# One V chunk per row kept in PSUM between the two passes of a decode kernel (GQA attention and MLP, twice)

## Chip, cores, metric

The kernel runs on one core of a Trainium2 chip. The metric is the device time of one execution in microseconds (us). The kernel before took 1153.25 us (median of 4 runs, 1149.37 to 1156.13).

## The reference, cut to what matters

```
B, Sq, D = 8, 1, 448;  Hq, Hkv, Sk, Dh = 16, 8, 4096, 256
x = x + A(layernorm(x), k_cache, v_cache, wq, wo)   # attention over the cache
x = x + Bmlp(layernorm(x), ...)
x = x + A(layernorm(x), k_cache, v_cache, wq, wo)   # the same cache again
x = x + Bmlp(layernorm(x), ...)
```

One K cache and one V cache of 8 rows x 8 heads x 4096 x 256 in bf16 are used twice, with another x. A row's K or V is 16.8 MB, more than the 15 slots (15.7 MB) that the kernel has beside the weights, so most of the cache is read from HBM twice. What a kernel can keep of a row between its first and second pass need not be read again. Here a chunk is 1.049 MB (128 partitions x 4096 bf16); a row has four head pairs `gp`, each with four K and four V chunks.

## The kernel before

Terms: PE is the matrix engine (PEld its weight loads), DVE the vector engine, ACT the scalar engine, SPq the queue that issues the loads. SBUF is the on-chip memory that loads land in, PSUM the banks that PE writes its sums to. "Scores" is q times K, PV the softmax weights times V; pass 0 and pass 1 are the two attentions over a row.

The kernel has 15 chunk slots in SBUF. Eleven chunks of a row stay there between the passes; the tasks of neighbouring rows are interleaved so that pass 1 of row b runs shortly after its kept chunks were loaded.

```python
NC = 15
kept = [(GP - 1, kv, n) for n in range(4) for kv in range(2)] + [(GP - 2, 0, n) for n in range(3)]
...
for b in range(Bn):
    tasks += [(1, b, gp) for gp in keep[::-1]]         # pass 1, pairs 3, 2: frees the kept slots
    if b + 1 < Bn:
        tasks += [(0, b + 1, gp) for gp in keep]       # pass 0, pairs 2, 3: fills them again
    ...
    tasks += [(1, b, gp) for gp in free]               # pairs 0, 1: four slots rotate
    if b + 2 < Bn:
        tasks += [(0, b + 2, gp) for gp in free]       # (cut: the first and last rows differ)
```

The chunks are handled one after the other, K chunk c of task n beside V chunk c of the task before. A slot is given to the next load in order as soon as its chunk has been used:

```python
if kv == 0:
    if not (ps == 1 and stays(it)):
        transpose_k(slot)            # two DVE transposes, 128x1024 uint32, in place
    step(idx)                        # a piece of a row's chain: wo, MLP, next q
    scores(sc_t[n % 2], slot, c, st["q"], gp)
    ...
    if c == 3:
        exps(p_n, sc_t[n % 2], st["z"], gp)     # one exp over a whole score bank
else:
    pv(st["o"], slot, c, gp, begin=...)         # st["o"]: one of three output banks
if not (ps == 0 and stays(it)):
    places.append(p)
emit_loads()
```

All eight PSUM banks are in use: two for scores, three for outputs, `misc`, and two for the sums of the rows' chains.

## Time and profile before

Lines of the page: first the busy time of an engine (share of the span, instructions), then the rate in 40 equal slices of the span, the DMA queue's packets, bytes and share, the bytes from HBM, and the chain of work that ended last, by engine and by line.

```profile
span 1149.6 us, 36707 instructions
PE 705.3 (61%) x17177; PEld 514.0 (45%) x17177; DVE 548.2 (48%) x904; ACT 113.9 (10%) x234; POOL 15.6 (1%) x25
...
GB/s 352 375 420 420 407 385 399 418 412 383 414 420 400 385 399 419 420 403 406 409 420 420 400 400 413 420 420 387 402 412 420 408 371 412 420 410 355 410 420 153
...
q1 hardware_dynamic: 68198, 455.19, 98.0%
...
HBM read 455.15 MB, written 0.01 MB: 396 GB/s over the span
...
DMA 69%; PE 13%; DVE 11%; SPq 3%; issue 2%; POOL 1%; ACT 0%; POOLq 0%; DVEq 0%; ACTq 0%
...
slot<-in_A_v_cache_dram SPq DMA_DIRECT2D x224, 1024.0 KB, 12.3
slot<-in_A_k_cache_dram SPq DMA_DIRECT2D x200, 1024.0 KB, 16.4
```

No compute engine is near full, the queue's packets fill 98% of the span, and the chain is DMA for 69% of it. The rate, however, swings: about 420 GB/s, then down to 371 to 414, once per row (about 137 us, five slices). The same as windows around row 3: the first from the first scores of pass 1, pair 3, to those of pair 1, the second from there to the next row's. The columns are the window, its length, the engines' busy time, the granted clock, the DMA share and GB/s.

```profile
562.60:637.40 74.80, 43.65 (x1072) 30.00 (x1073) 32.88 (x37) 8.52 (x17) 0.00 (x0) 0.57 1.01 418
637.40:699.40 62.00, 42.09 (x970) 31.14 (x969) 33.75 (x69) 5.56 (x12) 1.25 (x2) 0.50 1.00 398
```

I call them the deep and the shallow stretch. In the deep one the kept slots come free one after the other and loads run ahead; in the shallow one 11 slots are held and four rotate. Counted from the issues and landings in the trace (a landing that isn't recorded is taken from its neighbours), up to 8 loads are in flight in row 3's deep stretch and 3 or 4 in its shallow one. The Trainium skill ("HBM Reference", section "Specifications") gives about 425 GB/s for a core that streams alone; the 416 to 426 of this trace's deep 10 us windows agree. My reading of the shallow rate, which e7 and e10 below test, is that the four slots' own cycle sets it. Four pieces of the chain that ended last, in order of time (start, length, what):

```profile
660.56 6.98 DMA slot<-in_A_k_cache_dram
667.56 2.38 DVE slot L547 x2
...
670.63 7.78 DMA slot<-in_A_k_cache_dram
678.43 2.37 DVE slot L547 x2
```

A K load lands 6.98 us after its issue, the two transposes take 2.38, the scores' rest and the semaphores 0.69 (667.56 + 2.38 to 670.63), and then the next load goes into a free slot. One turn is 10.07 us. Four chunks in 10.07 us would be 417 GB/s; any further delay of PE or DVE in the turn lowers that: 398 GB/s, the rate of this stretch, is a turn of 10.5 us on average.

The groups that matter for the change (line, engine, operation, tiles, shapes, count; busy us, mean ns; idle before it and what ended that):

```profile
L547 DVE STREAM_TRANSPOSE slot<-slot 128x1024 uint32<-128x1024 uint32 x400 | 472.7, 1222 | 383.7 <-DMA slot<-in_A_k_cache_dram 375.0
L555 PE MATMUL sc<-slot,qbd 128*8 128x128 bf16 x8192 | 280.6, 286 | 345.6 <-DVE slot L547 287.2
...
L564 ACT ACTIVATE p_n<-sc 128x512 bf16<-128x512 f32 x64 | 84.7, 1323 | 780.6 <-PE sc L555 780.6
...
L381 PE MATMUL misc<-zm,one 128*128 128x8 f32 (+1 forms) x66 | 18.1, 348 | 6.7 <-ACT ptw L584 6.7
```

The DVE waits for K loads (375.0 us), the scores for the DVE. In the last line the z matmul waits for an ACT copy of other columns of `misc`: in this program a wait covers the PSUM bank as a whole.

### The profile page before, as it was taken

What the parts mean: (1) busy time and instruction counts of PE and PEld (TensorE: products, weight loads), DVE (VectorE), ACT (ScalarE), POOL (GpSimd) and SP (SyncE); (2) the same over time, 40 slices, a digit from 0 to 9 for tenths busy, and PEclk for the clock granted to TensorE, in tenths of its full rate; (3) what the DMA queues carried; (4) which work ended last, traced back from release to release, by engine and by line L of the source; (5) the groups of instructions that cost most, each with busy time, mean ns of one, the idle gap of its engine ahead of it and who ended that gap; (6) DMA issues with size and microseconds to landing.
All of it is one profiled execution on the core that took longest, in us unless ns stands there. A gap on an engine that the chain in (4) does not pass through costs nothing.

```text
span 1149.6 us, 36707 instructions
## 1 busy us (share of the span) xinstructions
PE 705.3 (61%) x17177; PEld 514.0 (45%) x17177; DVE 548.2 (48%) x904; ACT 113.9 (10%) x234; POOL 15.6 (1%) x25
## 2 busy tenths in 40 slices
PE   3144677457755667456764676646665576647787
PEld 2023455345533455344542454425443365425666
DVE  5145453455354544546254553445534553445352
ACT  0001011100110011001110101010011001100100
POOL 0000000000000000000000000000000000000000
PEclk9999997655655556555565557555575556555655
DMA  9999999999999999999999999999999999999993
GB/s 352 375 420 420 407 385 399 418 412 383 414 420 400 385 399 419 420 403 406 409 420 420 400 400 413 420 420 387 402 412 420 408 371 412 420 410 355 410 420 153
DMA packets 68349, 457.52 MB, mean 398 GB/s; under 512 B 6999, under 2 KB 13030, under 8 KB 13542
## 3 DMA queue, kind: packets, MB, share of 16 engines
q1 hardware_dynamic: 68198, 455.19, 98.0%
q8 instruction: 134, 2.20, 0.8%
q14 instruction: 17, 0.14, 0.0%
HBM read 455.15 MB, written 0.01 MB: 396 GB/s over the span
## 4 chain that ended last, share of the span: by engine, by line
DMA 69%; PE 13%; DVE 11%; SPq 3%; issue 2%; POOL 1%; ACT 0%; POOLq 0%; DVEq 0%; ACTq 0%
DMA slot<-in_A_k_cache_dram 62%; DVE slot L547 9%; DMA slot<-in_A_v_cache_dram 6%; PE sc L555 4%; PE o L596 3%; PE y_ps L318 2%; SPq L148 2%; PE q_ps L274 1%; DMA wq_sb<-in_A_wq_dram 1%; SPq L539 1%; PE o L610 1%; DVE qbd L300 1%; PE o L318 1%; PE h_ps L336 0%; PE misc L381 0%
## 5 line engine op out<-in xcount | busy, mean ns | idle before, releaser
L547 DVE STREAM_TRANSPOSE slot<-slot 128x1024 uint32<-128x1024 uint32 x400 | 472.7, 1222 | 383.7 <-DMA slot<-in_A_k_cache_dram 375.0
L555 PE MATMUL sc<-slot,qbd 128*8 128x128 bf16 x8192 | 280.6, 286 | 345.6 <-DVE slot L547 287.2
L555 PEld LDWEIGHTS <-qbd 128*8 128x8 bf16 x8192 | 194.5, 105 | 430.8 <-issue 298.6
L596 PE MATMUL o<-slot,ptw 128*8 128x256 bf16 x3968 | 242.8, 388 | 55.8 <-DMA slot<-in_A_v_cache_dram 33.9
L564 ACT ACTIVATE p_n<-sc 128x512 bf16<-128x512 f32 x64 | 84.7, 1323 | 780.6 <-PE sc L555 780.6
L596 PEld LDWEIGHTS <-ptw 128*8 128x8 bf16 x3968 | 107.9, 109 | 93.8 <-issue 45.0
L318 PEld LDWEIGHTS <-wo_sb 128*128 128x128 bf16 (+1 forms) x1600 | 64.8, 124 | 16.2 <-issue 15.6
L318 PE MATMUL y_ps<-OT,wo_sb 128*128 128x1 bf16 (+1 forms) x1280 | 55.5, 177 | 1.5 <-issue 1.5
L384 DVE RECIPROCAL rz<-misc 128x8 f32<-128x8 f32 (+1 forms) x33 | 6.4, 193 | 96.3 <-PE misc L381 96.3
L274 PEld LDWEIGHTS <-wq_sb 128*128 128x128 bf16 x1152 | 33.9, 104 | 19.1 <-issue 17.3
L274 PE MATMUL q_ps<-xb,wq_sb 128*128 128x1 bf16 (+1 forms) x1152 | 35.3, 166 | 11.4 <-DMA wq_sb<-in_A_wq_dram 3.6
L584 ACT CAST ptw<-misc 128x128 bf16<-128x128 f32 x64 | 17.5, 274 | 211.9 <-PE misc L577 159.4
L411 PEld LDWEIGHTS misc<-R,o_sb 128*128 128x128 f32 x124 | 25.9, 293 | 11.0 <-issue 11.0
L318 PEld LDWEIGHTS <-w_sb 128*128 128x128 bf16 (+1 forms) x630 | 25.7, 125 | 7.3 <-issue 5.2
L411 PE MATMUL misc<-R,o_sb 128*128 128x8 f32 x124 | 28.8, 343 | 0.0
L232 POOL TENSOR_TENSOR t<-t,nhalf 128x2 f32<-128x2 f32 (+1 forms) x17 | 10.7, 630 | 1075.8 <-DVE t L239 978.0
L318 PE MATMUL y_ps<-HT_t,w_sb 128*128 128x1 bf16 (+1 forms) x560 | 24.2, 177 | 0.5 <-DVE HT_t L359 0.5
L300 DVE TENSOR_SCALAR qbd<-misc,quad 128x64 bf16<-128x64 f32 x64 | 13.8, 278 | 22.0 <-PE misc L294 22.0
L381 PE MATMUL misc<-zm,one 128*128 128x8 f32 (+1 forms) x66 | 18.1, 348 | 6.7 <-ACT ptw L584 6.7
L336 PEld LDWEIGHTS <-w_sb 128*128 128x128 bf16 x560 | 17.2, 105 | 9.6 <-issue 9.2
L336 PE MATMUL h_ps<-xb,w_sb 128*128 128x1 bf16 (+1 forms) x560 | 17.9, 166 | 4.9 <-DVE xb L249 4.6
L381 PEld LDWEIGHTS misc<-zm,one 128*128 128x128 f32 x66 | 15.2, 287 | 11.9 <-ACT ptw L584 8.4
(92 smaller groups left out, 207.7 us busy)
## 6 DMA issues: line engine op xcount, KB each, us to landing
slot<-in_A_v_cache_dram SPq DMA_DIRECT2D x224, 1024.0 KB, 12.3
slot<-in_A_k_cache_dram SPq DMA_DIRECT2D x200, 1024.0 KB, 16.4
wo_sb<-in_A_wo_dram SPq DMA_DIRECT2D x1, 3584.0 KB, 26.6
wq_sb<-in_A_wq_dram SPq DMA_DIRECT2D x3, 1024.0 KB, 7.0
w_sb<-in_B_w_dram SPq DMA_DIRECT2D x1, 1568.0 KB, 12.8
w_sb<-in_B_w_dram SPq DMA_DIRECT2D x3, 448.0 KB, 26.8
wq_sb<-in_A_wq_dram SPq DMA_DIRECT2D x2, 256.0 KB, 10.0
w_sb<-in_B_w_dram SPq DMA_DIRECT2D x2, 112.0 KB, 9.0
```

The source lines that it names most:

```text
L148: nc.sync.dma_start(t[:, fc * cols : (fc + 1) * cols], src[fc * 128 : fc * 128 + 128, :])
L274: nc.tensor.matmul(q_ps[:, j * Hq + h, :], w, xbs(nb)[:, xi, :], start=(fc == 0), stop=(fc == 3),)
L300: nc.vector.tensor_scalar_mul(qbd[:, :, :, a, :], qs.rearrange("p e (f g u h) -> p (e f) u g h", f=2, u=2, h=2)[:, :, u], quad[:, a : a + 1],)
L318: nc.tensor.matmul(r, w[:, i, lo:hi], rhs(i), start=(first and fc == 0 and i == rows[0]), stop=(stop and i == rows[-1]), skip_group_check= ...
L336: nc.tensor.matmul(h_ps[:, c * nb : c * nb + nb], w, xbs(nb)[:, xi, :], start=(fc == 0), stop=(fc == 3),)
L381: nc.tensor.matmul(z_ps, ones, zm[:], start=True, stop=True)
L411: nc.tensor.matmul(ot_ps[:, j], o_sb[:, 128 * j : 128 * j + 128], R[:], start=True, stop=True)
L547: nc.vector.transpose(w, w)
L555: nc.tensor.matmul(sc[32 * k : 32 * k + 8, 128 * x : 128 * x + 128], qbd[:, ep, gp].rearrange("p a h -> p (a h)"), kv[:, k, 2 * half + e2, ...
L564: nc.scalar.activation(p_sb[:].rearrange("p t i x -> p x t i"), sc[:].rearrange("p (x t i) -> p x t i", x=4, t=4), ACT.Exp, scale=scale_ex ...
L584: nc.scalar.copy(ptw[:, :, :, 6:8], pt_ps.rearrange("p t k (a h) -> p a (t k) h", a=4),)
L596: nc.tensor.matmul(o_ps[32 * q : 32 * q + 8, 256 * (g // 4) : 256 * (g // 4) + 256], ptw[:, a, 4 * (y % 4) + y // 4, w : w + 8], v[:, y * ...
```

## The change

A twelfth chunk of each row, V chunk 1 of pair 2, is kept as well: after its PV in pass 0, four DVE transposes move it into four PSUM banks, and in pass 1 four more bring it back into a slot, so it need not be loaded twice. (Transposing the same blocks twice is meant to give the data back.) For that the other uses of PSUM shrink to four banks: one score bank with exp in two halves, two output banks (one per half row) in place of three, and the chains' sums in columns of `misc`. The diff, cut to its core (helpers' new arguments, and the last rows' use of the store banks, are left out):

```diff
+    inner = (GP - 2, 1, 1)
-    sc_t = [ps_s.tile([128, 512], FP32, name=f"sc{n}") for n in range(2)]
-    o_banks = [ps_o.tile([128, 512], FP32, name=f"o{n}") for n in range(3)]
+    sc = psum.tile([128, 512], FP32, name="sc")
+    o_banks = [psum.tile([128, 512], FP32, name=f"o{n}") for n in range(2)]
+    store = [psum.tile([128, 512], FP32, name=f"store{n}") for n in range(4)]
+    def room_ps(what, nb):
+        at, n = {"y": (320, 8), "st": (336, 2), "h": (352, HC), "q": (384, NB2)}[what]
+        if nb == 1:
+            return misc[:, at : at + n]
+        ...                                    # several rows at once: store[0] or store[1]
-    loads = [it for it in items if not (tasks[it[0]][0] == 1 and stays(it))]
+    loads = [it for it in items if not (tasks[it[0]][0] == 1 and (stays(it) or inside(it)))]
+    def away(slot):
+        for n in range(4):
+            nc.vector.transpose(
+                store[n][:].bitcast(U32), slot[:].bitcast(U32)[:, 512 * n : 512 * n + 512]
+            )
+    def back(slot):
+        for n in range(4):
+            nc.vector.transpose(
+                slot[:].bitcast(U32)[:, 512 * n : 512 * n + 512], store[n][:].bitcast(U32)
+            )
     ...
-            if c == 3:
+            if c == 1:
                 p_n = work.tile([128, 4, 32, 4], BF16, tag="p_sb", bufs=1)
                 p_of[n] = p_n
-                exps(p_n, sc_t[n % 2], st["z"], gp)
+            if c % 2 == 1:
+                exps(p_of[n], st["z"], gp, c // 2)
+            if (ps, gp, c) == (1, keep[-1], 1):
+                where[(b, inner[0]), inner[1:]] = kept_place
+                back(slots[kept_place])
     ...
-                pv(st["o"], slot, c, gp, begin=(ps, b) not in begun)
+                if ("o", g8) not in st:
+                    while len(in_use) == 2:
+                        step(10 * len(items))
+                    st["o", g8] = ...          # a free one of the two output banks
+                pv(st["o", g8], slot, c, gp, begin=(ps, b, g8) not in begun)
+                if ps == 0 and inside(it):
+                    away(slot)
     ...
         if not (ps == 0 and stays(it)):
-            if final and stays(it) and at_end is not None:
+            if (ps, gp, kv, c) == (1, keep[-1], 0, 0):
+                kept_place = p                 # this slot is withheld for the way back
+            elif final and stays(it) and at_end is not None:
```

More of the change, by code (lines that the diff above doesn't have):

```diff
@@ L68 @@
     chn = ctx.enter_context(tc.tile_pool(name="chn", bufs=1))
-    ps_s = ctx.enter_context(tc.tile_pool(name="ps_s", bufs=1, space=bass.MemoryType.PSUM))
-    ps_t = ctx.enter_context(tc.tile_pool(name="ps_t", bufs=1, space=bass.MemoryType.PSUM))
-    ps_o = ctx.enter_context(tc.tile_pool(name="ps_o", bufs=1, space=bass.MemoryType.PSUM))
-    ps_m = ctx.enter_context(tc.tile_pool(name="ps_m", bufs=1, space=bass.MemoryType.PSUM))
+    psum = ctx.enter_context(tc.tile_pool(name="psum", bufs=1, space=bass.MemoryType.PSUM))
     ctx.enter_context(tc.manual_schedule())
@@ L113 @@
     nc.vector.memset(ptw[:], 0.0)
-    misc = ps_t.tile([128, 512], FP32, name="misc")
-    ot_bank = misc[:, 256:384]
-    bank = ["chain"]
-    sc_t = [ps_s.tile([128, 512], FP32, name=f"sc{n}") for n in range(2)]
-    o_banks = [ps_o.tile([128, 512], FP32, name=f"o{n}") for n in range(3)]
-    for t in sc_t + o_banks:
-        nc.vector.memset(t[:], 0.0)
+    misc = psum.tile([128, 512], FP32, name="misc")
+    ot_bank = misc[:, 256:320]
+    sc = psum.tile([128, 512], FP32, name="sc")
+    o_banks = [psum.tile([128, 512], FP32, name=f"o{n}") for n in range(2)]
+    store = [psum.tile([128, 512], FP32, name=f"store{n}") for n in range(4)]
+    for t in [sc] + o_banks:
+        nc.vector.memset(t[:], 0.0)
+    def room_ps(what, nb):
+        at, n = {"y": (320, 8), "st": (336, 2), "h": (352, HC), "q": (384, NB2)}[what]
+        if nb == 1:
+            return misc[:, at : at + n]
+        at, n = {"y": (0, 8), "st": (64, 2), "h": (80, HC), "q": (256, NB2)}[what]
+        return store[0 if nb == Bn else 1][:, at : at + n * nb]
     wv = consts.tile([128, 4], FP32, name="wv")
@@ L175, in rows_to_cols @@
         idn = identb[:nb, :nb]
-        ps = ps_m.tile([128, 4, nb], FP32, tag=bank[0])
+        ps = room_ps("y", nb)[:, 0 : 4 * nb].rearrange("p (f b) -> p f b", b=nb)
         for fc in range(3):
@@ L210, in norm @@
         yield
-        st = ps_m.tile([128, 2, nb], FP32, tag=bank[0])
-        nc.tensor.matmul(st[:], ones, xs, start=True, stop=True)
+        st = room_ps("st", nb).rearrange("p (s b) -> p s b", b=nb)
+        nc.tensor.matmul(st, ones, xs, start=True, stop=True)
         yield
         mv = room("mv", (1, 2), 528)[:, 0]
-        nc.vector.tensor_copy(mv, st[:])
+        nc.vector.tensor_copy(mv, st)
         var = room("var", (1, 1), 608)[:, 0, 0]
@@ L268, in project_q @@
         yield from norm(xT[:, :, b0 : b0 + nb], nb, False)
-        q_ps = ps_m.tile([128, NB2, nb], FP32, tag=bank[0])
+        q_ps = room_ps("q", nb).rearrange("p (c b) -> p c b", b=nb)
         for j in range(2):
@@ L282, in project_q @@
                     yield
-        nc.vector.tensor_copy(qT, q_ps[:])
+        nc.vector.tensor_copy(qT, q_ps)
         yield
@@ L304, in spread_q, with y_room, add_cols @@
             )
+    def y_room(nb):
+        return room_ps("y", nb).rearrange("p (u f b) -> p u f b", u=2, b=nb)
     def out_cols(rhs, w, n, b0, nb, every):
-        y_ps = ps_m.tile([128, 4, nb], FP32, tag=bank[0])
-        yield from add_cols(y_ps, rhs, w, range(n), nb, every)
+        y_ps = y_room(nb)[:, 0]
+        yield from add_cols(y_ps, rhs, w, range(n), every)
         xs = xT[:, :, b0 : b0 + nb]
-        nc.vector.tensor_add(xs, xs, y_ps[:])
-    def add_cols(y_ps, rhs, w, rows, nb, every, first=True, stop=True):
+        nc.vector.tensor_add(xs, xs, y_ps)
+    def add_cols(y_ps, rhs, w, rows, every, open=None):
         for fc in range(5):
@@ L317, in add_cols @@
             for i in rows:
+                if open is None:
+                    start, stop = i == rows[0], i == rows[-1]
+                else:
+                    start = open[0] and fc == 0 and i == rows[0]
+                    stop = open[1] and i == rows[-1]
                 nc.tensor.matmul(
@@ L321, in add_cols @@
                     rhs(i),
-                    start=(first and fc == 0 and i == rows[0]),
-                    stop=(stop and i == rows[-1]),
-                    skip_group_check=True,
+                    start=start,
+                    stop=stop,
+                    skip_group_check=open is not None,
                 )
@@ L331, in mlp_hidden @@
         yield from norm(xT[:, :, b0 : b0 + nb], nb, True)
-        h_ps = ps_m.tile([128, HC * nb], FP32, tag=bank[0])
+        h_ps = room_ps("h", nb)
         for c in range(HC):
@@ L352, in mlp_hidden @@
             HT = scratch(256, HC * nb // 2).bitcast(BF16).rearrange("p (c b) -> p c b", b=nb)
-        nc.vector.tensor_scalar_mul(hh, h_ps[:], 0.5)
-        nc.vector.scalar_tensor_tensor(g0, hh, 2 * 0.044715, h_ps[:], ALU.mult, ALU.mult)
-        nc.vector.scalar_tensor_tensor(g0, g0, 1.0, h_ps[:], ALU.add, ALU.mult)
+        nc.vector.tensor_scalar_mul(hh, h_ps, 0.5)
+        nc.vector.scalar_tensor_tensor(g0, hh, 2 * 0.044715, h_ps, ALU.mult, ALU.mult)
+        nc.vector.scalar_tensor_tensor(g0, g0, 1.0, h_ps, ALU.add, ALU.mult)
         nc.scalar.activation(g0, g0, ACT.Tanh, scale=0.7978845608028654)
@@ L372, in z_cols @@
         zm = chn.tile([128, 4, np_], FP32, tag=f"zm{np_}")
+        zs_t = chn.tile([128, 2], FP32, tag="zs")
+        zs = zs_t[:, 0:np_]
+        nc.vector.tensor_add(
+            zs, zall[:, 0, gps[0] : gps[-1] + 1], zall[:, 1, gps[0] : gps[-1] + 1]
+        )
         nc.vector.tensor_tensor(
             zm[:],
-            zall[:, gps[0] : gps[-1] + 1].unsqueeze(1).to_broadcast([128, 4, np_]),
+            zs.unsqueeze(1).to_broadcast([128, 4, np_]),
             usel[:].unsqueeze(2).to_broadcast([128, 4, np_]),
@@ L406, in half @@
         o_sb = chn.tile([128, Dh], FP32, tag="o_sb")
-        nc.scalar.copy(o_sb[:], o_ps[:, Dh * g8 : Dh * g8 + Dh])
+        nc.scalar.copy(o_sb[:], o_ps[:, 0:Dh])
+        in_use.remove(o_ps)
         yield
-        ot_ps = ot_bank[:, 64 * g8 : 64 * g8 + 16].rearrange("p (j h) -> p j h", j=2)
+        ot_ps = ot_bank[:, 32 * g8 : 32 * g8 + 16].rearrange("p (j h) -> p j h", j=2)
         for j in range(2):
@@ L416, in half @@
         yield
-    def add_half(y_ps, OT, g8, nb, first, every):
-        yield from add_cols(
-            y_ps,
-            lambda i: OT[:, i % 2, i // 2],
-            wo_sb,
-            range(16 * g8, 16 * g8 + 16),
-            nb,
-            every,
-            first=first,
-            stop=not first,
-        )
+    in_use = []
     def first_half(b, st):
         OT = work.tile([128, 2, Hq, 1], BF16, tag="OT", bufs=1)
-        y_ps = ps_m.tile([128, 4, 1], FP32, tag="chain")
-        st["OT"], st["y"] = OT, y_ps
-        yield from half(st["o"], st["z"], 0, OT[:, :, :, 0])
-        yield from add_half(y_ps, OT, 0, 1, True, 2)
-    def chain(b, st):
-        OT, y_ps = st["OT"], st["y"]
-        yield from half(st["o"], st["z"], 1, OT[:, :, :, 0])
-        yield from add_half(y_ps, OT, 1, 1, False, 2)
+        st["OT"] = OT
+        yield from half(st["o", 0], st["z"], 0, OT[:, :, :, 0])
+        yield from add_cols(
+            y_room(1)[:, 0], lambda i: OT[:, i % 2, i // 2], wo_sb, range(NB2 // 2), 2
+        )
+    def chain(b, st):
+        OT = st["OT"]
+        yield from half(st["o", 1], st["z"], 1, OT[:, :, :, 0])
+        yield from add_cols(
+            y_room(1)[:, 1], lambda i: OT[:, i % 2, i // 2], wo_sb, range(NB2 // 2, NB2), 2
+        )
         xs = xT[:, :, b : b + 1]
-        nc.vector.tensor_add(xs, xs, y_ps[:])
+        nc.vector.tensor_add(xs, xs, y_room(1)[:, 0])
+        nc.vector.tensor_add(xs, xs, y_room(1)[:, 1])
         yield from mlp(b, 1)
@@ L452, in first_last @@
     def first_last(b, st):
-        yield from half(st["o"], st["z"], 1, OT2[:, :, :, b])
+        yield from half(st["o", 1], st["z"], 1, OT2[:, :, :, b])
         if b == Bn - 1:
-            yield from add_half(st["y"], OT2[:, :, :, b : b + 1], 1, 1, claim(st), 2)
+            yield from add_cols(
+                st["y"],
+                lambda i: OT2[:, i % 2, i // 2, b : b + 1],
+                wo_sb,
+                range(NB2 // 2, NB2),
+                2,
+                open=(claim(st), False),
+            )
     def claim(st):
@@ L462, in last @@
     def last(b, st):
-        yield from half(st["o"], st["z"], 0, OT2[:, :, :, b])
+        yield from half(st["o", 0], st["z"], 0, OT2[:, :, :, b])
     def rest(b, st):
@@ L472, in rest @@
         yield
-        o_row = ps_m.tile([nb, D], FP32, tag=bank[0])
+        o_row = store[0][:nb, 0:D]
         for fc in range(4):
@@ L480, in rest @@
         xo = scratch(1024, D // 2).bitcast(BF16)[:nb]
-        nc.vector.tensor_copy(xo, o_row[:])
+        nc.vector.tensor_copy(xo, o_row)
         nc.sync.dma_start(out[:nb].rearrange("b s d -> (b s) d"), xo)
@@ L514, in stays, with inside @@
         return (tasks[n][2], kv, c) in kept
-    loads = [it for it in items if not (tasks[it[0]][0] == 1 and stays(it))]
+    def inside(it):
+        n, kv, c = it
+        return (tasks[n][2], kv, c) == inner
+    loads = [it for it in items if not (tasks[it[0]][0] == 1 and (stays(it) or inside(it)))]
     places = list(range(NC))
@@ L547, in transpose_k, with scores @@
             nc.vector.transpose(w, w)
-    def scores(sc, t, x, qbd, gp):
+    def scores(t, x, qbd, gp):
         kv = t[:].rearrange("p (k t e i r) -> p k e r t i", k=4, t=4, e=4, r=2)
@@ L561, in scores, with exps @@
                 )
-    def exps(p_sb, sc, zall, gp):
+    def exps(p_sb, zall, gp, u):
         nc.scalar.activation(
-            p_sb[:].rearrange("p t i x -> p x t i"),
-            sc[:].rearrange("p (x t i) -> p x t i", x=4, t=4),
+            p_sb[:, :, :, 2 * u : 2 * u + 2].rearrange("p t i x -> p x t i"),
+            sc[:, 256 * u : 256 * u + 256].rearrange("p (x t i) -> p x t i", x=2, t=4),
             ACT.Exp,
             scale=scale_exp,
-            accum_out=zall[:, gp : gp + 1],
+            accum_out=zall[:, u, gp : gp + 1],
         )
+    def away(slot):
+        for n in range(4):
+            nc.vector.transpose(
+                store[n][:].bitcast(U32), slot[:].bitcast(U32)[:, 512 * n : 512 * n + 512]
+            )
+    def back(slot):
+        for n in range(4):
+            nc.vector.transpose(
+                slot[:].bitcast(U32)[:, 512 * n : 512 * n + 512], store[n][:].bitcast(U32)
+            )
     def transpose_p(p_sb):
@@ L596, in pv @@
             nc.tensor.matmul(
-                o_ps[32 * q : 32 * q + 8, 256 * (g // 4) : 256 * (g // 4) + 256],
+                o_ps[32 * q : 32 * q + 8, 0:256],
                 ptw[:, a, 4 * (y % 4) + y // 4, w : w + 8],
@@ L624 @@
     ps0 = rows_to_cols(x_row, Bn)
-    nc.vector.tensor_copy(xT[:], ps0[:])
+    nc.vector.tensor_copy(xT[:], ps0)
     emit_loads(5)
@@ L647, in step @@
         for kind in ("chain", "last"):
-            bank[0] = kind
             e = next((e for e in gens if e["kind"] == kind), None)
@@ L666 @@
         ps, b, gp = tasks[n]
-        p = where[(b, gp), (kv, c)] if ps == 1 and stays(it) else where[it]
+        p = where[(b, gp), (kv, c)] if ps == 1 and (stays(it) or inside(it)) else where[it]
         slot = slots[p]
@@ L681 @@
                 st["q"] = qbd
-            if "o" not in st:
-                z_t = chn.tile([128, GP], FP32, tag="zall", bufs=3)
-                st["o"], st["z"] = o_banks[0], z_t
-                o_banks.append(o_banks.pop(0))
+            if "z" not in st:
+                z_t = chn.tile([128, 2, GP], FP32, tag="zall", bufs=3)
+                st["z"] = z_t
                 if final:
-                    st["y"] = o_banks[0][:, 0:4].unsqueeze(2)
-                    oc = st["o"][:, 0 : 2 * Hq].rearrange("p (j h) -> p j h", j=2)
+                    st["y"] = store[2][:, 0:4].unsqueeze(2)
+                    oc = store[3][:, 0 : 2 * Hq].rearrange("p (j h) -> p j h", j=2)
             if not (ps == 1 and stays(it)):
@@ L691 @@
             step(idx)
-            scores(sc_t[n % 2], slot, c, st["q"], gp)
-            if c == 0 and n > 0:
+            scores(slot, c, st["q"], gp)
+            if c == 0 and n - 1 in p_of:
                 transpose_p(p_of.pop(n - 1))
-            if c == 3:
+            if c == 1:
                 p_n = work.tile([128, 4, 32, 4], BF16, tag="p_sb", bufs=1)
                 p_of[n] = p_n
-                exps(p_n, sc_t[n % 2], st["z"], gp)
+            if c % 2 == 1:
[3 more added lines that the diff above has]
+                back(slots[kept_place])
         else:
             st = state[ps, b]
-            if n in p_of:
+            if c == 0 and n in p_of:
                 transpose_p(p_of.pop(n))
@@ L718 @@
                             range(h0, h0 + 4),
-                            1,
                             5,
-                            first=claim(st),
-                            stop=(gp == free[-1] and u == 1),
+                            open=(claim(st), gp == free[-1] and u == 1),
                         )
@@ L725 @@
             else:
-                pv(st["o"], slot, c, gp, begin=(ps, b) not in begun)
-                begun.add((ps, b))
+                g8 = gp // 2
+                if ("o", g8) not in st:
+                    while len(in_use) == 2:
+                        step(10 * len(items))
+                    st["o", g8] = next(t for t in o_banks if all(t is not u for u in in_use))
+                    in_use.append(st["o", g8])
+                pv(st["o", g8], slot, c, gp, begin=(ps, b, g8) not in begun)
+                begun.add((ps, b, g8))
+                if ps == 0 and inside(it):
+                    away(slot)
             if c == 3:
@@ L753 @@
         step(10 * len(items))
-    bank[0] = "last"
     xs = xT[:, :, Bn - 1 : Bn]
@@ L761 @@
     W = D // 4
-    o_row = ps_m.tile([128, W], FP32, tag="chain")
-    nc.vector.memset(o_row[:], 0.0)
+    o_row = store[0][:, 0:W]
+    nc.vector.memset(o_row, 0.0)
     HT = run(mlp_hidden(Bn - 1, 1))
@@ L788 @@
     xo = spare[1][:, 256 : 256 + W]
-    nc.vector.tensor_copy(xo, o_row[:])
+    nc.vector.tensor_copy(xo, o_row)
     nc.sync.dma_start(
```

## The prediction

> **What bounds the kernel.** The DMA queue. Its packets took 98.0% of the 16 engines' span, 455 MB (DMA-queue part of the page); the chain that ended last is 69% DMA, 62% K loads. PE is 61% busy, DVE 48%. In 10 us windows the rate alternates, once per row (about 137 us):
> - stretch A, many loads issued ahead: 419 to 424 GB/s, so one 1.049 MB chunk costs 2.50 us. The Trainium skill, "HBM Reference", Specifications, gives about 425 GB/s for a core streaming alone; the trace agrees.
> - stretch B, while 11 of the 15 slots hold a row's kept chunks and only 4 rotate: 375 to 410, twice near 330. Here the slot's cycle limits: a load takes about 7 us to land, then K's two DVE transposes (2.37 us), scores (about 1 us), next issue (chain of waits, timeline).
> - from about 1080 us on: the chain is PE work, no longer DMA (chain in order of time).
>
> **What the change removes.** One V load per row: counted in program order, 424 chunk loads become 416, 8.4 MB of 455 (1.8%). It goes from stretch A, at 2.50 us. The last row's falls into the PE-bound end, so I count 7: 17.5 us.
>
> **What it adds and moves.**
> 1. Four 128x512 transposes out, four back, per row. The 128x1024 one takes 1222 ns; estimate 0.62 us each, 2.5 us a group. Out comes where about 10 loads are ahead; back comes where DVE idles about 10 us (699 to 709 us: kept K needs no transpose). Nearly free.
> 2. The chunk needs a slot when it returns. The first kept slot freed in pass 1 is withheld, so loads ahead run 4,4,5,6,7 where they ran 4,5,6,7,8. The ramp from B to A is one chunk later: estimate 0.5 us per row, 4 us.
> 3. One score bank instead of two; exp in halves (64 of 1.32 us become 128 of about 0.7). PE must wait for the half exp, but a PV of about 1 us lies between, and K scores cannot follow each other faster than 2.37 us. About 1 us.
> 4. The row chain's sums move into the misc bank. The Trainium skill, "PSUM — Partial Sum Buffer", Terms, says that two engines may not be on one bank and quadrant at once. The trace agrees: the z matmul waits for the ACT copy of other columns of misc (6.7 us, 16 times). More such waits, in B, where a PE delay reaches the slot's cycle: estimate 0.4 us per row, 3 us.
> 5. Two output banks instead of three. In the first rows and rows 5 to 7 one stays open, so the next pair waits for the last one's copy: 7 pairs at about 0.3 to 0.5 us, 2 to 3 us.
>
> Sum: -17.5 + 4 + 1 + 3 + 2.5 = -7 us, or down to -15 if my losses are too high. **Predicted 1144 us, range 1133 to 1153.** Chances: faster by over 2% 0.07, within 2% 0.9, slower 0.03.
>
> **What would show it.** V issues 216 instead of 224, HBM read 446.8 MB; A still at 420 and about 2.5 us shorter per row; B as long or 0.5 to 1.5 us longer; 64 new transposes near 0.62 us; the PE end after the last B unchanged within 2 us.
>
> **What would make it wrong.** If waits on the single score bank or misc stretch B by 2 us per row, the gain is gone (about 1155). If B doesn't suffer and the end shortens too: about 1135.

## The result

The changed kernel took 1138.28 us (median of 4 runs, 1135.72 to 1138.73), the kernel before 1153.25. The ratio is 0.9868, 95% interval 0.9831 to 0.9905: 1.3% faster, inside 2%. Measured once more in later rounds (experiment e5) it was 0.9907, 0.9887 to 0.9928. A ratio is the mean time of one kernel's fast runs over that of the other's fast runs of the same rounds, so it isn't quite the ratio of the medians. A difference in us below is the ratio's distance from 1 times the mean of the kernel before in those rounds.

The lines of the page of the changed kernel that answer to those above:

```profile
span 1133.7 us, 36989 instructions
PE 704.3 (62%) x17177; PEld 509.5 (45%) x17177; DVE 593.8 (52%) x1007; ACT 124.3 (11%) x362; POOL 15.6 (1%) x25
...
GB/s 350 369 421 420 413 369 384 418 417 377 404 419 412 395 398 419 420 408 391 410 419 420 407 393 395 420 419 386 412 418 420 406 379 407 419 417 370 412 419 93
...
q1 hardware_dynamic: 67046, 446.80, 97.6%
...
HBM read 446.77 MB, written 0.01 MB: 394 GB/s over the span
...
DMA 63%; PE 15%; DVE 13%; issue 4%; SPq 3%; ACT 1%; POOL 1%; POOLq 0%; DVEq 0%; ACTq 0%
...
slot<-in_A_v_cache_dram SPq DMA_DIRECT2D x216, 1024.0 KB, 10.9
slot<-in_A_k_cache_dram SPq DMA_DIRECT2D x200, 1024.0 KB, 14.1
```

Eight V loads and 8.38 MB are gone, and the shape of the rate is the same: 420 in the deep slices, 369 to 413 in the shallow ones. Row 3, in the same two stretches:

```profile
556.90:629.10 72.20, 43.14 (x1072) 29.48 (x1072) 38.19 (x47) 9.35 (x27) 0.00 (x0) 0.59 1.01 418
629.10:692.50 63.40, 42.38 (x970) 30.78 (x970) 34.26 (x71) 6.00 (x18) 1.25 (x2) 0.50 0.99 392
```

The deep stretch is 2.6 us shorter at the same 418 GB/s: one chunk at 2.50 us. The shallow stretch isn't shorter. The new DVE work is in the deep stretch (38.19 us busy against 32.88). The groups:

```profile
L569 DVE STREAM_TRANSPOSE slot<-slot 128x1024 uint32<-128x1024 uint32 x400 | 472.8, 1222 | 337.1 <-DMA slot<-in_A_k_cache_dram 322.6 <-PE o L632 13.3
L577 PE MATMUL sc<-slot,qbd 128*8 128x128 bf16 x8192 | 277.5, 286 | 322.9 <-DVE slot L569 260.3 <-issue 23.9 <-DVE zs_t L389 8.6
...
L586 ACT ACTIVATE p_n<-sc 128x256 bf16<-128x256 f32 x128 | 95.6, 747 | 736.7 <-PE sc L577 736.5
...
L604 DVE STREAM_TRANSPOSE slot<-store 128x512 uint32<-128x512 uint32 x32 | 20.1, 685 | 7.6 <-PE sc L577 7.6
L597 DVE STREAM_TRANSPOSE store<-slot 128x512 uint32<-128x512 uint32 x32 | 20.0, 694 | 1.2 <-DMA slot<-in_A_v_cache_dram 1.0
...
L400 PE MATMUL misc<-zm,one 128*128 128x8 f32 x62 | 17.1, 350 | 7.4 <-ACT ptw L620 7.4
```

Waits that the smaller PSUM makes new or longer (who waited, for whom: us in total, times, longest):

```profile
PE sc L577 <- ACT p_n L586: 6.8, 15, 0.8
...
PE misc L216 <- DVE t L211: 2.2, 6, 1.0
...
PE misc L350 <- ACT ptw L620: 1.6, 4, 0.4
...
PE misc L332 <- ACT ptw L620: 1.2, 3, 0.4
PE misc L431 <- ACT o_sb L426: 1.1, 1, 1.1
```

So PE waited for the single score bank in 15 places, 6.8 us in the whole span. The chain's matmuls at L350 and L332 waited 2.8 us for the ACT copy of other columns of `misc`; the lines of L216 and L431 are waits for an operand (`t`, `o_sb`), not for the bank. The Trainium skill ("PSUM — Partial Sum Buffer", section "Terms") says that two engines may not be on one bank and quadrant (a group of 32 partitions) at the same time; the waits for `sc` and `misc` fit that, and no run here breaks the rule to see what happens.

**A ledger.** The packets in the trace give, for each kernel, the bytes moved after the first 52 us (the weights) and the time of the last chunk's packet. I split the span into the start, the time that the remaining bytes need at 420 GB/s, what the stream takes beyond that ("lost"), and the tail after the last packet. One profiled run each, in us; the later kernels are explained below.

| kernel | start | bytes at 420 GB/s | lost in the stream | tail | span |
|---|---|---|---|---|---|
| before | 52 | 1040.0 (436.8 MB) | 41.7 | 16.0 | 1149.6 |
| after | 52 | 1020.2 (428.5 MB) | 41.0 | 20.4 | 1133.7 |
| e5, after once more | 52 | 1019.9 (428.4 MB) | 46.0 | 19.1 | 1137.1 |
| e2, load dropped only | 52 | 1020.0 (428.4 MB) | 37.9 | 19.6 | 1129.4 |
| e7, five slots + store | 52 | 1040.7 (437.1 MB) | 20.8 | 17.9 | 1131.4 |
| e10, five slots, no store | 52 | 1060.0 (445.2 MB) | 19.2 | 14.6 | 1145.8 |

Before to after: 19.8 us of bytes go, the loss stays in this trace (in e5, another trace of the same kernel, it is 5 us larger: so much does one profiled run scatter), and the tail grows by 4.4 us. My reading is that the end is PE work that doesn't become shorter when its last loads come earlier. The other traces fit: with four rotating slots the tail is 18.6 to 20.6 us in all seven kernels without the V load, and 16.0 to 17.4 in the four with it.

### The profile page after: what moved, and what is told of

Its sections match the earlier page's. It is cut to its first block, busy times and chain, and to the rows that moved or that the text cites. A ratio compares the mean times of both kernels' runs of the same rounds, so it can differ in the third digit from the quotient of the medians.

```text
span 1133.7 us, 36989 instructions
## 1 busy us (share of the span) xinstructions
PE 704.3 (62%) x17177; PEld 509.5 (45%) x17177; DVE 593.8 (52%) x1007; ACT 124.3 (11%) x362; POOL 15.6 (1%) x25
## 4 chain that ended last, share of the span: by engine, by line
DMA 63%; PE 15%; DVE 13%; issue 4%; SPq 3%; ACT 1%; POOL 1%; POOLq 0%; DVEq 0%; ACTq 0%
DMA slot<-in_A_k_cache_dram 59%; DVE slot L569 11%; PE sc L577 5%; DMA slot<-in_A_v_cache_dram 4%; PE o L632 3%; SPq L152 2%; PE misc L332 2%; PE store L332 1%; DMA wq_sb<-in_A_wq_dram 1%; SPq L561 1%; PE misc L350 1%; PE store L646 1%; DVE qbd L304 1%; ACT p_n L586 0%; PE misc L278 0%
## 5 line engine op out<-in xcount | busy, mean ns | idle before, releaser
L569 DVE STREAM_TRANSPOSE slot<-slot 128x1024 uint32<-128x1024 uint32 x400 | 472.8, 1222 | 337.1 <-DMA slot<-in_A_k_cache_dram 322.6
L577 PE MATMUL sc<-slot,qbd 128*8 128x128 bf16 x8192 | 277.5, 286 | 322.9 <-DVE slot L569 260.3
L577 PEld LDWEIGHTS <-qbd 128*8 128x8 bf16 x8192 | 188.5, 105 | 409.6 <-issue 214.6
L586 ACT ACTIVATE p_n<-sc 128x256 bf16<-128x256 f32 x128 | 95.6, 747 | 736.7 <-PE sc L577 736.5
L332 PEld LDWEIGHTS <-wo_sb 128*128 128x128 bf16 (+1 forms) x1600 | 64.2, 123 | 15.1 <-issue 14.2
L332 PE MATMUL misc<-OT,wo_sb 128*128 128x1 bf16 (+1 forms) x1280 | 55.1, 176 | 2.5 <-issue 2.5
L278 PE MATMUL misc<-xb,wq_sb 128*128 128x1 bf16 x1024 | 31.6, 165 | 5.6 <-DVE xb L253 3.4
L586 ACT ACTIVATION_READ_ACCUMULATOR p_n<-sc 128x1 f32 x128 | 33.7, 264 | 0.0
L431 PEld LDWEIGHTS misc<-R,o_sb 128*128 128x128 f32 x124 | 26.7, 300 | 12.3 <-issue 10.3
L332 PEld LDWEIGHTS <-w_sb 128*128 128x128 bf16 (+1 forms) x630 | 26.7, 125 | 11.9 <-issue 11.3
L431 PE MATMUL misc<-R,o_sb 128*128 128x8 f32 x124 | 29.6, 349 | 1.1 <-ACT o_sb L426 1.1
L332 PE MATMUL misc<-HT_t,w_sb 128*128 128x1 bf16 (+1 forms) x560 | 24.5, 177 | 3.1 <-issue 1.3
L236 POOL TENSOR_TENSOR t<-t,nhalf 128x2 f32<-128x2 f32 (+1 forms) x17 | 10.7, 630 | 1060.1 <-DVE t L243 965.0
L604 DVE STREAM_TRANSPOSE slot<-store 128x512 uint32<-128x512 uint32 x32 | 20.1, 685 | 7.6 <-PE sc L577 7.6
L350 PEld LDWEIGHTS <-w_sb 128*128 128x128 bf16 x560 | 17.5, 104 | 13.4 <-issue 12.9
L400 PE MATMUL misc<-zm,one 128*128 128x8 f32 (+1 forms) x66 | 18.3, 350 | 7.4 <-ACT ptw L620 7.4
```

Source lines behind the costliest of these rows:

```text
L278: nc.tensor.matmul(q_ps[:, j * Hq + h, :], w, xbs(nb)[:, xi, :], start=(fc == 0), stop=(fc == 3),)
L332: nc.tensor.matmul(r, w[:, i, lo:hi], rhs(i), start=start, stop=stop, skip_group_check=open is not None,)
L350: nc.tensor.matmul(h_ps[:, c * nb : c * nb + nb], w, xbs(nb)[:, xi, :], start=(fc == 0), stop=(fc == 3),)
L400: nc.tensor.matmul(z_ps, ones, zm[:], start=True, stop=True)
L431: nc.tensor.matmul(ot_ps[:, j], o_sb[:, 128 * j : 128 * j + 128], R[:], start=True, stop=True)
L569: nc.vector.transpose(w, w)
```

## The experiments

All of them were measured in five rounds against the kernel before. They ran in three groups, each on another chip: e1 to e4, e5 to e8, e9 to e12. Within a group I compare the kernels' own times, with a 95% interval from the scatter of these runs; across groups only ratios to the kernel before. Three of them (e2, e3, e4) compute with wrong data in that V chunk; the comparison with the reference still passed them: wrong data in one of the 16 V chunks of a row's second pass evidently move the output by less than its tolerance. So a pass of this comparison doesn't show by itself that the chunk's way through PSUM is right.

My theory after the result: only the bytes count (theory 1). Rivals: the prediction's ledger, in which the layout and the withheld slot cost about 10 us together (theory 2); and that the new layout itself brings a part of the gain (theory 3).

### e1: the layout without the store

```diff
     def inside(it):
-        return (tasks[n][2], kv, c) == inner
+        return False
     # and no back(), no withheld slot
```

> The changed PSUM layout alone (one score bank, half exps, two output banks, chain in the misc bank), no chunk stored: all 424 chunk loads are made again, HBM read 455 MB. Theory 1 (only the bytes count; the layout is hidden behind the DMA): within 2 us of before, 1151 to 1155 us. Theory 2 (the prediction's ledger: the layout costs about 6 us, hidden in the sum by something else): 1157 to 1161 us. Theory 3 (the layout itself brings a part of the gain, by shorter exps and an earlier chain): 1145 to 1149 us.

Measured: 1155.47 us, ratio 1.0036 (1.0010 to 1.0063): 4.1 us slower than before, 1.2 to 7.3. Theory 3 falls: the layout brings nothing, it costs. The estimate of the prediction for its three parts was 6.5 us.

### e2: the load dropped in the kernel before, nothing else

```diff
+    loads = [... if not (tasks[it[0]][0] == 1 and (stays(it) or inside(it)))]
+    # PV of that chunk reads the slot of V chunk 2, wrong on purpose
+    p = ... else where[(n, kv, c + (ps == 1 and inside(it)))]
```

> The kernel before, with the V load of pass 1 left out and that PV reading the neighbour chunk's slot: a wrong result on purpose; nothing else is changed. Theory 1: 7 loads of 2.50 us come off before the end that PE bounds, 17 to 18 us, 1135 to 1137 us; 20 us if the last row's load counts as well. Theory 2: the same 17 to 18 us. Theory 3: less than 14 us, 1140 us or more, since the layout would bring the rest.

Measured: 1133.74 us, ratio 0.9841 (0.9816 to 0.9866): 18.3 us faster, 15.4 to 21.2. This is the price of the loads by themselves, and it agrees with seven loads of 2.50 us (17.5); eight (20.0) lie in the interval as well. That the eighth is given back at the end is read from the tail, 19.6 us where it was 16.0.

### e3: the changed kernel without its transposes

```diff
-                back(slots[kept_place])
-                if ps == 0 and inside(it):
-                    away(slot)
```

> The changed kernel without the transposes out and back; the slot is withheld as before and holds old K values, so the result is wrong on purpose. If the transposes are hidden (theories 1 and 3): as the changed kernel, within 1 us of 1138. If they are on the path in some rows: 2 to 5 us faster than it, 1133 to 1136 us.

Measured: 1136.14 us, ratio 0.9872 (0.9842 to 0.9902). The changed kernel has 0.9868 and 0.9907 in its two measurements, both on other chips, so no difference is seen, but only to some 4 us. e8 below is the sharper test.

### e4: the changed layout, load dropped, nothing moved, no slot withheld

```diff
-                kept_place = p
-                back(slots[kept_place])   # and no away()
+    p = ... else where[(n, kv, c + (ps == 1 and inside(it)))]   # wrong on purpose
```

> The changed layout with the load left out, no transposes and no slot withheld (PV reads the neighbour's slot, wrong result on purpose): all of the gain, none of the cost of keeping the chunk. Theory 1: within 2 us of the changed kernel, about 1136 us. Theory 2: the withheld slot costs about 4 us, so 1134 us or less. The difference to the run without transposes is the price of the slot that is withheld, to the run with only the load dropped it is the price of the layout.

Measured: 1137.45 us, ratio 0.9879 (0.9850 to 0.9907). Against e3 (slot withheld, 0.9872) nothing is gained (e3 minus e4: -0.7 us, -5.1 to 3.6): the withheld slot costs less than these runs can tell. Against e2, which differs only by the layout, it is 0.0038 of the time of before slower, 4.4 us (1.2 to 7.3 from the two kernels' own times). That is the 4.1 us of e1 once more, found in another pair of kernels. And the parts add up: -18.3 (e2) + 4.1 (e1) = -14.2, measured here -13.9 (0.0121 x 1151.3). Theory 2 holds in kind and not in size: layout and withheld slot together, e3 against e2, cost 3.6 us (-0.5 to 7.6), where it has about 10.

### e5: the changed kernel again

> The changed kernel once more, as the control of this chip and these rounds: all theories say 0.987 of before, 15 us less.

Measured: 1139.66 us, ratio 0.9907 (0.9887 to 0.9928), 10.7 us faster than before: less than the 15.2 of the first measurement, the intervals overlap. It is the control for e6 to e8, which ran in the same rounds.

### e6: the slot withheld later

```diff
-            if (ps, gp, kv, c) == (1, keep[-1], 0, 0):
+            if (ps, gp, kv, c) == (1, keep[-1], 1, 0):
                 kept_place = p
     # back() moved from K chunk 1 to V chunk 1 of that pair
```

> The changed kernel with the withheld slot and the way back moved later in pass 1: the slot of the first kept V chunk of the last pair is withheld in place of that of its first kept K chunk, and the transposes back come eight chunk steps before use less. Loads ahead then climb 4, 5, 6, 7, 8 as in the kernel before. If the late ramp costs what the prediction put on it (0.5 us per row): 3 to 4 us faster than the changed kernel. If it costs nothing: the same within 1 us.

Measured: 1137.64 us, ratio 0.9884 (0.9865 to 0.9903), 2.6 us less than e5 (0.0023 x 1150.5). The interval of the difference is -0.6 to 6.0, and e4 against e3 showed no such gain, so this stays unsettled: none is shown, and the prediction's 4 us isn't excluded here.

### e7: the store pays for a slot, not for a load

```diff
-    kept = [...] + [(GP - 2, 0, n) for n in range(3)]
+    kept = [...] + [(GP - 2, 0, n) for n in range(2)]
```

> The changed kernel with one K chunk less kept per row, so that five slots rotate in place of four while the kept chunks sit; the chunk in PSUM then pays for a slot and not for a load: 424 loads, 455 MB again. If shallow stretches lose little (theory 1: the bytes are what counts): 0 to 5 us faster than the kernel before, so slower than the changed kernel by 10 us or more. If the four-slot cycle is what loses most (the rate of 350 to 400 GB/s there against 420): equal to the changed kernel or faster.

One K chunk less is kept in SBUF, so five slots rotate in the shallow stretches and 424 chunks are loaded, as before the change. Measured: 1134.22 us, ratio 0.9850 (0.9833 to 0.9868), correct. It beats the kernel before and the changed kernel (0.9907, 0.9887 to 0.9928 in the same rounds; 6.4 us between their own times, 3.6 to 9.3), though it reads as much as the kernel before. Theory 1, "only the bytes count", falls here. The page's rate and bytes, and row 3 in the same two stretches:

```profile
GB/s 348 366 420 419 420 395 401 418 421 413 408 418 421 414 417 418 420 411 408 420 418 422 404 416 417 420 420 403 416 419 420 415 390 420 419 421 402 413 418 125
...
HBM read 455.15 MB, written 0.01 MB: 402 GB/s over the span
```

```profile
554.70:629.50 74.80, 44.07 (x1074) 29.95 (x1075) 40.39 (x49) 9.29 (x27) 0.00 (x0) 0.57 1.01 420
629.50:689.10 59.60, 42.26 (x970) 30.66 (x970) 34.34 (x71) 6.00 (x18) 1.25 (x2) 0.50 1.01 410
```

The shallow stretch runs at 410 GB/s in place of 392, with 4 or 5 loads in flight in place of 3 or 4, and is 3.8 us shorter; the deep one has its load back and is 2.6 us longer. In the ledger 20.8 us are lost in place of 41.0. The times also scatter less: 1131.60 to 1134.36 over five runs, where the changed kernel spread over 1136.55 to 1143.92 in the same rounds. In the means of rows 2 to 4 of the profiled runs:

| kernel | deep stretch, us | shallow stretch, us |
|---|---|---|
| before | 74.9 | 61.4 |
| e1, layout only | 75.3 | 62.8 |
| e2, load dropped only | 72.8 | 60.8 |
| e4, layout and load dropped | 72.5 | 62.4 |
| after | 72.4 | 61.7 |
| e7, five slots | 74.8 | 59.6 |
| e10, five slots, no store | 77.3 | 59.7 |

The deep stretch shortens by a load wherever the load is dropped. With four slots the shallow one is 1.4 to 1.6 us longer in e1 against before and in e4 against e2, and 0.9 in the changed kernel against e2. Single rows scatter by up to 3 us, so this is a hint of where the layout's 4 us lie, not more. With five slots it is the same in both layouts (59.6 and 59.7 us).

### e8: the transposes doubled

```diff
-        for n in range(4):
+        for n in (0, 1, 2, 3) * 2:      # in away() and in back()
```

> The changed kernel with each transpose out and back done twice: 64 more of about 0.69 us, 44 us more of DVE work. If they are hidden: within 1 us of the changed kernel. If they lie on the path in full: 44 us slower; in part, a few us, and then in the shallow stretches and after the last row's.

Measured: 1138.53 us, ratio 0.9896 (0.9875 to 0.9918), not slower than e5 (0.9907): -1.3 us, -4.9 to 2.3, for 38 us more of DVE work in the trace. Twice the moves cost nothing that can be seen, so the moves are hidden. The trace of the changed kernel shows why for the way back of row 4 (start, length, instruction, idle before it):

```profile
693.56 2.51 DVE L604 STREAM_TRANSPOSE slot<-store 128x512 uint32<-128x512 uint32 x4 [0.97 <-PE sc L577]
...
695.24 1.18 SPq L561 DMA_DIRECT2D slot<-in_A_k_cache_dram  x2
```

The DVE had nothing else to do (it had been idle for 0.97 us), as the K chunks of this part are kept ones and already transposed, and loads went on being issued meanwhile.

### e9: five slots and the slot withheld later

The edits of e6 and e7 together.

> Both versions that came out ahead of the changed kernel together: five rotating slots (10 kept chunks in SBUF, one in PSUM, 424 loads) and the withheld slot taken later. If the late ramp is worth about 2 us where five slots rotate too: about 0.983 of before, 1131 us. If the late ramp matters only with four slots: as with five alone, 0.985, 1134 us.

Measured: 1132.31 us, ratio 0.9846 (0.9814 to 0.9878), correct; no different from e7's 0.9850 on another chip. With five slots the later place brings nothing that shows. This is the fastest kernel by its median (1132.04 to 1134.10), on a par with e7.

### e10: five slots in the kernel before

The edit of e7 in the kernel before: nothing in PSUM, 432 chunk loads.

> The kernel before, nothing in PSUM, with one K chunk less kept per row: five slots rotate, 432 loads, 463.5 MB. If a fifth slot is worth about 21 us wherever it comes from (five rotating slots against the layout alone: 17.2 + 4.1 us), and 8 loads more cost 17 to 20 us: 1 to 4 us faster than before, the same within noise. If a fifth slot is worth less than the bytes (theory 1): slower than before by 8 us or more. If the gain of the five-slot kernel came from the layout together with the store: slower by 15 us or more.

Measured: 1148.02 us, ratio 0.9982 (0.9949 to 1.0015): the same as before within noise, with 8.39 MB more to read.

```profile
HBM read 463.54 MB, written 0.01 MB: 405 GB/s over the span
```

In the ledger it pays 20.0 us for the bytes, loses 22.5 us less in the stream (19.2 in place of 41.7), and its tail is 1.4 us shorter: -3.9, and its span is 3.8 us shorter. So a fifth rotating slot is worth as much as eight loads, with the old PSUM layout too. That bears out the reading that the four-slot cycle held the shallow rate down: five chunks in the turn of 10.5 us would be about 500 GB/s (an estimate), more than the 420 or so that the stream reaches at best. Between e10 and e7 (0.9982 and 0.9850) the store drops eight loads again, and that brings 15 us again; so does e9, in the rounds of e10 (15.6 us, 14.4 to 16.9).

### e11 and e12: what of the layout costs

e11 gives e1 two score banks again, e12 moves the chains' sums out of `misc` into a bank of their own; both use banks that store nothing in e1.

```diff
     # e11
+    sc_t, cur = [sc, store[2]], [0]       # scores and exps use sc_t[n % 2]
     # e12
-            return misc[:, at : at + n]
+            return store[1][:, at : at + n]
```

> The layout alone (first experiment, 4 us slower than before), with two score banks again, exps still in halves; the second bank is one of the four that store nothing there. If the single score bank is what costs: within 1 us of before. If the shared misc bank, or two output banks in place of three, cost: still 3 to 4 us slower than before.

> The layout alone, with the chain's sums out of the misc bank into a bank of their own (again one that stores nothing there). If sharing the misc bank is what costs: within 1 us of before. If the single score bank or the two output banks cost: still 3 to 4 us slower than before.

Measured: e11 1155.91 us, ratio 1.0041 (1.0003 to 1.0079); e12 1153.61 us, ratio 1.0032 (0.9997 to 1.0067). Neither gives back visibly the 0.0036 that e1 lost. In the traces the waits aimed at are gone: PE's waits for ACT on a score bank fall from 6.2 us (e1) to 1.6 (e11), and those of L350 and L332 for the copy from `misc`, 2.8 us in e1, don't occur in e12. But both intervals reach down to within 0.4 us of before, so these runs don't exclude either bank as the cause. What they do add: all three kernels that have the layout without the store (e1, e11, e12) read 1.003 to 1.004 of the kernel before, on two chips. What is left of the layout's edits is two output banks with chain steps pulled forward, the exps in halves (which e11 and e12 keep), and the extra sum of the two halves' denominators. They were not tried apart; which of them costs stays open.

## Why the prediction was right, point by point

The time was predicted as 1144 us (1133 to 1153), within 2%; it came out as 1138 and 1140, within 2%.

Being in the range is a weak test: it reaches from no gain at all (1153) to more than the whole price of the loads. The mechanism is tested by the parts. Its losses summed to 10.5 us; measured, against the 18.3 of e2, they are 3.1 (first measurement) or 7.6 (e5), in other rounds than e2's: smaller than predicted, and on which side of half is open.

- **The bytes, 17.5 us for seven loads**: right. The loads alone are worth 18.3 us (e2), and the deep stretch is shorter by one load per row in each kernel of the table that drops it and keeps four slots. That the eighth load's time would be lost in the PE-bound end fits the tail after the last packet, which grew from 16.0 to 20.4 us; the times alone don't tell seven loads from eight. From the first scores of the last row's pass 1 to the end it is 76.8 us before and 78.7 after, about the "unchanged within 2 us" that it named as a sign.
- **Transposes, 0.62 us each and nearly free**: 0.69 us each (the way out came with about 8 loads in flight, not the 10 it names), and free as far as is seen: taken away (e3) or doubled (e8), they make no difference.
- **The withheld slot, 4 us**: not shown. e3 against e4 shows nothing (at most 3.6 us), e6 against e5 2.6 us in an interval of -0.6 to 6.0. The slower ramp that it names is in the traces: in row 3 the loads in flight rise 3, 4, 5, 5, 6, 7, 7, 8 where they rose 4, 4, 5, 6, 6, 7, 8.
- **Layout, 1 + 3 + 2.5 us**: the sum is near, 4.1 and 4.4 us in two pairs of kernels. The parts are not shown: PE's direct waits for the score bank are 6.8 us in all, but two score banks (e11) and a bank of their own for the chains (e12) gave no gain that these runs can resolve.
- **"B as long or 0.5 to 1.5 us longer"**: it fits (61.4 and 61.7 us in rows 2 to 4, 62 and 63.4 in row 3).
- **What the prediction didn't ask**: it named the four-slot cycle as the limit of the shallow stretch, and then counted only what a dropped load brings. The same four banks, spent on a fifth rotating slot, bring more: 17.3 us against before (e7), where the changed kernel brings 10.7 in the same rounds. The layout alone costs 4.1 us, so the slot itself is worth about 21 us (17.3 + 4.1, an estimate), and the loads 18.3. e10, without the layout, gives about 20 (2.1 + 18.3).

## What to carry to other kernels

When a kernel streams through a few rotating buffers, split the loss against the full rate by stretches before spending new room: a buffer that stays resident saves its bytes once, but a further rotating buffer can save more if the rotation is too short for one turn of load, work and reissue. Here keeping the eleventh chunk in SBUF was worth no more than the slot that it took (e10), so what the last slot buys, a load less or a turn more, should be tried both ways. Data can be parked in free PSUM banks by an engine that idles at that moment, at no visible cost, but emptying the banks for it wasn't free. That the data come back unchanged needs a test of its own.

## What the Trainium skill lacked or had wrong

- "HBM Reference", section "Specifications": its figure of about 425 GB/s for a core alone held (416 to 426 in deep windows here), but I found no page that says how many 1 MiB loads must rotate to hold it. In these runs, where each K chunk also has 2.4 us of transposes and about 1 us of scores, four slots (3 or 4 loads in flight) gave 392 to 398 GB/s in row 3's shallow stretch and five (4 or 5 in flight) gave 410.
- "VectorE: DVE Perf Modes", section "The three transpose paths": its table names only SBUF as the place that the VectorE transpose goes to. Here it ran into PSUM and out of it, 694 and 685 ns for 128x512 uint32, beside 1222 ns for twice the elements from SBUF to SBUF.
- "PSUM — Partial Sum Buffer" treats PSUM as the matmul's accumulator; I found no page that tells of it as a parking place for 1 MB of bf16 data, moved in and out by the DVE. Here it held row 4's chunk from 595.6 to 693.6 us, and eight rows cost 40 us of DVE time in all, with no cost seen (e8). Whether it came back bit for bit was not checked by itself.
